# Clustered attention in front of two expert layers: four kinds of operands per head in place of six

## The chip, the cores and the metric

One core of a Trainium2 chip runs the whole program. The metric is the device time of one execution in microseconds (us). Engines: PE (TensorE, matrix products), DVE (VectorE), ACT (ScalarE), POOL (GpSimd), SP (SyncE, which here only issues DMAs).

## The reference

Attention of 2 batches x 8 heads, 768 positions, head size 64. Every query and key belongs to the one of 16 centroids with the largest cosine similarity; a query only sees keys of its own cluster. The result feeds a squared-ReLU layer (512 to 2048 to 512) and then a layer of 8 experts of which each token takes one.

```python
q_assign = argmax(q_n @ c_n.T)            # first of equal maxima
k_assign = argmax(k_n @ c_n.T)
mask = q_assign[:, :, :, None] == k_assign[:, :, None, :]
scores = where(mask, scale * q @ k.T, -1e9)
scores = scores - max(scores, -1)
attn = exp(scores); attn = attn / (sum(attn, -1) + 1e-9)
x = attn @ v
g = s * relu(x @ w_in) ** 2 + b ; y = g @ w_out
out[token] = gate * relu(y @ w1[e]) @ w2[e]     # e: the token's best expert
```

A query whose cluster holds no key has every score at -1e9. All its weights are then equal, and its result is the mean of all values.

## The kernel before

Numbers keep nearly float32 accuracy by being split into two f16 parts, high and low; a product is then three products of parts.

**One head** is prepared in two functions and used in two more. `prep1` (L133) splits K and Q: ACT casts the high parts into `pk1`, POOL subtracts to get the low parts, and a transposing DMA writes `tk1`, with [high; low] of K and of Q on the 128 rows. V is split into `v1` without a transpose. `prep2` (L188) computes similarities to the centroids on PE (`sim`, L198), and on DVE a one-hot row per position: maximum, comparison, weighting by descending index so that of equal maxima the first stays, maximum, comparison (L202 to L210). It then packs `pk2` with four kinds of rows: (0) K high with the keys' one-hot times 32768, (1) Q high twice, (2) Q high with a mask, (3) Q low with the mask. A matmul with ones counts the keys in each cluster (`cnt`, L216); a query whose cluster is empty gets a zero mask and its values are cleared by a bitwise and (L219 to L231), so that its scores come out equal. Kinds 0 to 2 are transposed to `tk2` (18 blocks of 128x128). With the two kinds of `tk1` that makes six.

`unit_max` (L243) computes, for half a head (384 queries), the scores with queries on partitions from high parts alone, in 6 matmuls of 128x384, and takes the row maximum on DVE (L255, L259). The maximum, scaled (L260), becomes one more column of kind 3, which is transposed to `qb`. `unit` (L266) computes for each of 6 key chunks the transposed scores from two accumulating matmuls, `tk1` with `tk2` kind 1 (L287) and `tk2` kind 0 with `qb` (L289); the maximum is subtracted in the second. ACT takes exponentials (L292 and, for chunks that are split into f16 parts, L297), POOL or DVE computes the low part `pl` (L300), and PE multiplies with V (L279). The DVE normalizes (L308 to L313), ACT and POOL write the result split in two (L316, L317).

**Transposes** go by DMA from SP's queue (L115), except for the first head and the centroids, which PE transposes by a product with an identity, in groups of three blocks, copied out alternately by ACT and DVE (L118 to L124).

**The order.** Generators are interleaved: while `unit` of head i walks its chunks, one step each of `unit_max` of head i+1 and `prep2` of head i+2 is issued, and `prep1` of head i+3. The weights of the squared-ReLU layer come as 64-bit numbers and are decoded in 32 chunks (`f64_chunk`: DVE L333, L334, L337, ACT L331, L339, POOL L340). The first chunks are held behind named instructions of head 0 and 1 with `issue_after`, which holds the chunk's instructions of the same engine as the named one; the rest are spread over heads 5 to 11. From head 8 on, steps of the squared-ReLU layer on batch 0 (`moe1`: PE L442 and L456, ACT L445 and L448, DVE L447 and L449) are issued between heads. When the heads are done, the rest of that layer runs, then the experts. The Tile framework puts instructions of each engine into an order by a simulation when it compiles; each engine then works in that order.

Of the kernel before, what the change touches and what calls it, by code (L numbers as in the profile page):

```python
# [43 lines left out]
def tile_kernel(ctx: ExitStack, tc, q, k, v, centroids, w_in, w_out, s, b, w_gate, w1, w2, out, dbg=None):  # L44
# [67 lines left out]
    def transpose(i, dst, src, pools=None):  # L112

        if i not in PE_T:
            nc.sync.dma_start_transpose(out=dst, in_=src.rearrange("p n x -> p (n x)"))  # L115
            return
        for g in range(0, src.shape[1], HC):
            pool, name = ((st_p, "st"), (sm_p, "sm"))[g // HC % 2] if pools is None else pools  # L118
            ps = pool.tile([P, HT], F32, name=name)
            nn = min(HC, src.shape[1] - g)  # L120
            for n in range(nn):
                nc.tensor.matmul(out=ps[:, n * P:(n + 1) * P], lhsT=src[:, g + n], rhs=ident, start=True, stop=True)
            (nc.scalar.copy if g // HC % 2 == 0 else nc.vector.tensor_copy)(
                out=dst[:, g:g + nn], in_=ps[:, 0:nn * P].rearrange("p (n x) -> p n x", n=nn))  # L124
# [8 lines left out]
    def prep1(i):  # L133
        h = hd[i]
        t = h.pop("kqv")
        kq = t[:, 0:2].rearrange("p a (c d) -> p (a c) d", d=D)
        pk1 = pk.tile([P, 2, NC, P], F16, name="pk1")
        kqp = pk1.rearrange("p a c x -> p (a c) x")
        nc.scalar.copy(out=kqp[:, :, 0:D], in_=kq)
        nc.gpsimd.tensor_tensor(out=kqp[:, :, D:2 * D], in0=kq, in1=kqp[:, :, 0:D], op=ALU.subtract)  # L140
        tk1 = tpool(i).tile([P, 2, NC, P], F16, name="tk1")
        transpose(i, tk1.rearrange("p a c x -> p (a c) x"), pk1.rearrange("p a c x -> p (a c) x"))
# [24 lines left out]
    _, wt_c = iota([P, C], [[-1, C]], C, 0, "wt_c")  # L167
# [20 lines left out]
    def prep2(i):  # L188
        bb, hh = heads[i]
        h = hd[i]  # L190
        pk1, tk1 = h.pop("pk1"), h["tk1"]
# [26 lines left out]
        ohq = tmp.tile([P, NC, C], F32, name="ohq")
        nc.vector.scalar_tensor_tensor(out=ohq, in0=cnt.unsqueeze(1).broadcast_to([P, NC, C]), scalar=0.0,  # L219
                                       in1=oh[:, NC:2 * NC], op0=ALU.is_gt, op1=ALU.mult)  # L220
        al = small.tile([P, NC], F32, name="al")
        nc.vector.tensor_reduce(out=al, in_=ohq, axis=AX.X, op=ALU.add)
        alm = small.tile([P, NC], I32, name="alm")
        nc.vector.tensor_scalar(out=alm, in0=al, scalar1=-1.0, scalar2=None, op0=ALU.mult)
        alb = small.tile([P, NC], F32, name="alb")
        nc.vector.tensor_scalar(out=alb, in0=al, scalar1=BIGM, scalar2=None, op0=ALU.mult)
        yield
        nc.vector.scalar_tensor_tensor(out=pk2[:, 2, :, 64:64 + C], in0=ohq, scalar=BIGM,
                                       in1=alb.unsqueeze(2).broadcast_to([P, NC, C]), op0=ALU.mult, op1=ALU.subtract)
        nc.vector.tensor_copy(out=pk2[:, 3, :, 64:64 + C], in_=pk2[:, 2, :, 64:64 + C])  # L230
        nc.vector.tensor_tensor(out=pk2.bitcast(I32)[:, 2:4, :, 0:D // 2],  # L231
                                in0=pk1.bitcast(I32)[:, 1].rearrange("p c (t d) -> p t c d", t=2),
                                in1=alm.unsqueeze(1).unsqueeze(3).broadcast_to([P, 2, NC, D // 2]),
                                op=ALU.bitwise_and)
        yield
# [665 lines left out]
```

## Time and profile before

| | us |
|---|---|
| runs before | 762.03, 757.33, 759.59 (median 759.59) |
| the profiled execution | 756.67 |
| its span in the profile | 754.9 |
| PE busy | 652.6 |
| DVE busy | 573.3 |
| ACT busy | 416.1 |
| POOL busy | 287.7 |
| mean granted clock of PE | 0.962 |

The durations come from one execution. Busy time of an engine is the union of its instructions' times; a matmul's duration holds its latency, so that means of single matmuls are longer than their share of the busy time. In a row of a group, "x16" is the number of instructions, then stand busy us and mean ns, then the idle time of the engine just before them and what ended it. Names such as `pk` stand for all tiles whose name begins so (pk1, pk2).

### The profile page before, as it was taken

Reading aid. Unit: us, or ns where it says so; the run is one execution under the profiler, and the core shown is the slowest. Engines: PE = TensorE matmul, PEld = TensorE weight load, DVE = VectorE, ACT = ScalarE, POOL = GpSimd, SP = SyncE. Lnnn points to the kernel's source line nnn. Section 1 sums busy time; section 2 is a strip of 40 time slices with the busy share of each in tenths; the row PEclk is TensorE's granted clock in tenths of the full one; section 3 lists DMA queues with packets and bytes.
Section 4 is the critical chain, followed back from the end, with each engine's and each line's share of the span. In section 5 each row is a group of like instructions: output and inputs, shape, how many; then the busy total and the mean of one; then the engine's idle time right before and its main releaser. Section 6 shows DMA issues by size and latency. Waiting matters only on the chain.

```text
span 754.9 us, 16103 instructions
## 1 busy us (share of the span) xinstructions
PE 652.6 (86%) x6171; PEld 424.4 (56%) x6171; DVE 573.3 (76%) x1271; ACT 416.1 (55%) x789; POOL 287.7 (38%) x335
## 2 busy tenths in 40 slices
PE   1467876988878889999999999999999889999884
PEld 1235654766544545566555565465476758776661
DVE  8999899979999997789862363276943867877772
ACT  5356566655677655566754252045713566756762
POOL 6346567645756545545434210011013323220101
PEclk9999699989998999999999999999999999999998
DMA  7465667656493345334201500008843378688841
GB/s 228 141 145 143 150 168 160 151 129 131 93 199 117 83 124 107 52 77 74 43 12 44 99 29 1 15 30 293 320 164 87 86 219 293 219 275 209 265 144 48
DMA packets 134482, 101.26 MB, mean 134 GB/s; under 512 B 110332, under 2 KB 116476, under 8 KB 132096
## 3 DMA queue, kind: packets, MB, share of 16 engines
q1 hardware_dynamic: 124304, 68.58, 36.9%
q10 hardware_dynamic: 6576, 22.06, 8.9%
q0 software_dynamic: 3520, 9.54, 3.5%
q8 instruction: 50, 0.82, 0.4%
q14 instruction: 32, 0.26, 0.1%
HBM read 85.05 MB, written 7.39 MB: 122 GB/s over the span
## 4 chain that ended last, share of the span: by engine, by line
PE 40%; DVE 28%; DMA 16%; issue 12%; ACT 2%; SPq 0%; POOLq 0%; POOL 0%; DVEq 0%; ACTq 0%
PE py L456 15%; PE ps L442 10%; DMA out<-o,oid 8%; DVE mxt L255 5%; PE pv L279 4%; PE hps L666 4%; DMA tk<-pk 3%; DVE l L334 2%; DVE r L447 2%; DVE l L333 2%; DVE m L337 2%; DMA raw<-in_moe_w_out 2%; PE st L289 2%; PE st L287 2%; PE sm L252 2%
## 5 line engine op out<-in xcount | busy, mean ns | idle before, releaser
L300 POOL TENSOR_TENSOR pl<-p,ph 128x384 f16<-128x384 f32 x128 | 127.1, 998 | 105.0 <-ACT ph L297 54.2
L442 PE MATMUL ps<-xt,wi 128*128 128x384 f16 x768 | 137.3, 331 | 0.0
L456 PE MATMUL py<-wo,g 128*128 128x512 f16 x576 | 134.0, 382 | 1.6 <-ACT r L445 1.6
L292 ACT ACTIVATE p<-st 128x384 f32<-128x384 f32 x192 | 93.6, 491 | 65.6 <-PE st L289 58.8
L255 DVE TENSOR_REDUCE mxt<-sm 128x1 f32<-128x384 f32 x192 | 102.2, 545 | 16.0 <-PE sm L252 15.5
L442 PEld LDWEIGHTS <-wi 128*128 128x128 f16 x768 | 74.7, 99 | 51.2 <-issue 4.7
L456 PEld LDWEIGHTS <-g 128*128 128x128 f16 x576 | 55.4, 98 | 63.2 <-issue 3.7
L252 PE MATMUL sm<-tk 128*128 128x384 f16 x192 | 64.0, 355 | 29.8 <-DVE mxt L255 27.2
L287 PE MATMUL st<-tk,tk 128*128 128x384 f16 x192 | 66.3, 345 | 7.1 <-ACT ph L297 5.1
L289 PE MATMUL st<-qb,tk 128*128 128x384 f16 x192 | 66.1, 347 | 6.6 <-DMA qb<-pk 6.6
L297 ACT ACTIVATE ph<-st 128x384 f16<-128x384 f32 x144 | 70.3, 489 | 0.0
L448 ACT ACTIVATE g<-r,b 128x384 f16<-128x384 f32 x64 | 39.4, 616 | 50.3 <-DVE r L447 50.3
L686 POOL DMA_INDIRECT out<-o,oid x16 | 22.2, 1385 | 106.3 <-ACT o L685 100.9
L680 PEld LDWEIGHTS <-ht 128*128 128x128 f16 x384 | 36.9, 98 | 42.6 <-issue 1.3
L449 DVE SCALAR_TENSOR_TENSOR g<-r,b,g 128x384 f16<-128x384 f32 x64 | 45.5, 710 | 18.5 <-ACT g L448 18.5
L279 PEld LDWEIGHTS <-ph 128*128 128x128 f16 x864 | 45.9, 101 | 21.9 <-issue 5.8
L523 POOL DMA_INDIRECT yreg<-yp,posi x12 | 12.5, 1042 | 113.1 <-DVE posi L509 87.3
L279 PE MATMUL pv<-v,ph 128*128 128x65 f16 x864 | 53.3, 198 | 1.9 <-ACT ph L297 1.4
L666 PE MATMUL hps<-x2t,wa 128*128 128x128 f16 x768 | 48.7, 227 | 7.0 <-DVE ht L671 4.4
L606 DVE SCALAR_TENSOR_TENSOR wa<-stg,wa 128x1024 f16<-128x1024 f32 x40 | 46.9, 1219 | 8.2 <-ACT wa L605 8.0
L666 PEld LDWEIGHTS <-wa 128*128 128x128 f16 x768 | 46.9, 102 | 9.7 <-issue 5.0
L447 DVE SCALAR_TENSOR_TENSOR r<-r,s 128x384 f32<-128x384 f32 x64 | 47.5, 742 | 1.6 <-ACT r L445 1.6
(219 smaller groups left out, 1264.4 us busy)
## 6 DMA issues: line engine op xcount, KB each, us to landing
stg<-in_moe_w SPq DMA_DIRECT2D x44, 1024.0 KB, 7.7
raw<-in_moe_w_out ACTq DMA_DIRECT2D x16, 512.0 KB
stg<-in_moe_w ACTq DMA_DIRECT2D x8, 1024.0 KB, 7.3
raw<-in_moe_w_in ACTq DMA_DIRECT2D x10, 512.0 KB, 6.0
kqv<-in_k SPq DMA_DIRECT2D x16, 192.0 KB, 3.7
kqv<-in_q SPq DMA_DIRECT2D x16, 192.0 KB, 3.9
kqv<-in_v SPq DMA_DIRECT2D x16, 192.0 KB, 5.6
raw<-in_moe_w_in SPq DMA_DIRECT2D x6, 512.0 KB, 6.1
```

The source lines that it names most:

```text
L252: nc.tensor.matmul(out=sm, lhsT=tk2[:, 2, c0 + c, :], rhs=tk2[:, 0, n * HC:(n + 1) * HC, :].rearrange("p c x -> p (c x)"), start=True, sto ...
L255: nc.vector.tensor_reduce(out=mxt[:, c, n:n + 1], in_=sm, axis=AX.X, op=ALU.max)
L279: nc.tensor.matmul(out=pv[:, c, :], lhsT=p[:, c * P:(c + 1) * P], rhs=w, start=first[0], stop=(kc == NC - 1 and c == HC - 1 and p is parts ...
L287: nc.tensor.matmul(out=st, lhsT=tk1[:, 0, kc, :], rhs=tk2[:, 1, c0:c0 + HC, :].rearrange("p c x -> p (c x)"), start=True, stop=False)
L289: nc.tensor.matmul(out=st, lhsT=tk2[:, 0, kc, :], rhs=qb.rearrange("p c x -> p (c x)"), start=False, stop=True)
L292: nc.scalar.activation(out=p32, in_=st, func=AF.Exp, scale=1.0 / 8.0)
L297: nc.scalar.activation(out=ph, in_=st, func=AF.Exp, scale=1.0 / 8.0)
L300: eng.tensor_tensor(out=pl, in0=p32, in1=ph, op=ALU.subtract)
L442: nc.tensor.matmul(out=ps, lhsT=wi[:, a, kk, f * P:(f + 1) * P], rhs=xt[:, c, kk], start=(kk == 0 and n == 0), stop=(kk == KD - 1 and n == 2))
L447: nc.vector.scalar_tensor_tensor(out=g0, in0=r, scalar=s4, in1=r, op0=ALU.mult, op1=ALU.mult)
L456: st8["py"] = nc.tensor.matmul(out=ps, lhsT=g[:, a, f, c * P:(c + 1) * P], rhs=wo[:, w, f], start=(f == 0 and n == 0), stop=(f == KF - 1 a ...
L666: nc.tensor.matmul(out=ps[:, j], lhsT=ws[:, w, kk * F + f0:kk * F + f0 + P], rhs=xt[:, a, kk], start=(i == 0), stop=(i == 3 * KD - 1))
```

## The change

Operands per head become four kinds: `tk1` holds, per chunk, [K high; K low] and [Q low; Q high], so that one pass gives both cross products; `tk2` holds K high and Q high with their one-hot rows (12 blocks). The high product, mask and maximum come in the second pass. Empty clusters are no longer treated ahead: `unit_max` derives a flag from the row maximum (no key reaches the level of an own cluster), and behind the normalization a predicated copy puts the mean of V, computed by a matmul with ones, into the rows that are flagged. The one-hot chain is in f16 and in one piece; scaling and copying into `pk2`, and the maximum's column, are ACT's. PE transposes write f16 in groups of six.

```diff
-    def transpose(i, dst, src, pools=None):
+    def transpose(i, dst, src, pool=None):
...
+        n0 = 2 * HC
+        for g in range(0, src.shape[1], n0):
+            nn = min(n0, src.shape[1] - g)
+            odd = g // n0 % 2
+            p, name = ((st_p, "st"), (sm_p, "sm"))[odd] if pool is None else pool
+            ps = p.tile([P, n0, P], F16, name=name)
             for n in range(nn):
-                nc.tensor.matmul(out=ps[:, n * P:(n + 1) * P], lhsT=src[:, g + n], rhs=ident, start=True, stop=True)
...
+                nc.tensor.transpose(out=ps[:, n], in_=src[:, g + n], identity=ident)
+            (nc.vector.tensor_copy if odd else nc.scalar.copy)(out=dst[:, g:g + nn], in_=ps[:, 0:nn])
...
-        pk1 = pk.tile([P, 2, NC, P], F16, name="pk1")
...
+        pk1 = pk.tile([P, NC, 4, D], F16, name="pk1")
+        nc.scalar.copy(out=pk1[:, :, 0::3], in_=kq)
+        nc.gpsimd.tensor_tensor(out=pk1[:, :, 1:3], in0=kq, in1=pk1[:, :, 0::3], op=ALU.subtract)
...
-        t = (pk if i < 2 else tpa).tile([P, 4, NC, P], F16, name=f"pk2_{i}", bufs=1)
+        t = (pk if i < 2 else tpa).tile([P, 2, NC, P], F16, name=f"pk2_{i}", bufs=1)
...
+        pk2 = pk2_of(i)
+        nc.scalar.copy(out=pk2[:, :, :, 0:D], in_=pk1[:, :, 0::3].rearrange("p c a d -> p a c d"))
...
-        oh = tmp.tile([P, 2 * NC, C], F32, name="oh")
+        oh = tmp.tile([P, 2 * NC, C], F16, name="oh")
...
-        st8[f"a{i}"] = nc.vector.tensor_scalar(out=pk2[:, 0, :, 64:64 + C], in0=oh[:, 0:NC], scalar1=BIGM, scalar2=None, op0=ALU.mult)
+        st8[f"a{i}"] = nc.vector.tensor_tensor(out=oh, in0=oh, in1=pm.unsqueeze(2).broadcast_to([P, 2 * NC, C]), op=ALU.is_equal)
+        nc.scalar.activation(out=pk2[:, 0, :, 64:64 + C], in_=oh[:, 0:NC], func=AF.Copy, scale=BIGM)
+        st8[f"b{i}"] = nc.scalar.activation(out=pk2[:, 1, :, 64:64 + C], in_=oh[:, NC:2 * NC], func=AF.Copy,
+                                            scale=BIGM, bias=-BIGM)
+        tk2 = tpool(i).tile([P, 2, NC, P], F16, name="tk2", bufs=4 if i < H else 2)
+        transpose(i, tk2.rearrange("p a c x -> p (a c) x"), pk2.rearrange("p a c x -> p (a c) x"))
         yield
...
+        vsp = aux.tile([P, D], F32, name="vsp", tag="aux")
         for c in range(NC):
-            nc.tensor.matmul(out=cnt, lhsT=ones16, rhs=pk2[:, 0, c, 64:64 + C], start=(c == 0), stop=(c == NC - 1))
...
+            for t in range(2):
+                nc.tensor.matmul(out=vsp, lhsT=ones16, rhs=v1[:, c, t, 1:1 + D], start=(c == 0 and t == 0), stop=(c == NC - 1 and t == 1))
+        vm = tmp.tile([P, D], F32, name="vm", bufs=3)
+        nc.scalar.activation(out=vm, in_=vsp, func=AF.Copy, scale=SX / S)
...
-                nc.tensor.matmul(out=sm, lhsT=tk2[:, 2, c0 + c, :],
+                nc.tensor.matmul(out=sm, lhsT=tk2[0:64 + C, 1, c0 + c, :],
...
-        st8[f"c{i}{qh}"] = nc.vector.tensor_scalar(out=pk2[:, 3, c0:c0 + HC, 64 + C], in0=mm1, scalar1=-1.0 / BIGM, scalar2=None,
+        st8[f"c{i}{qh}"] = nc.scalar.activation(out=pk2[:, 1, c0:c0 + HC, 64 + C], in_=mm1, func=AF.Copy, scale=-1.0 / BIGM)
...
+            nc.scalar.activation(out=h["flag"], in_=h["mm1"], func=AF.Relu, scale=-1.0, bias=nokey)
...
-            nc.tensor.matmul(out=st, lhsT=tk1[:, 0, kc, :],
...
+            nc.tensor.matmul(out=st.rearrange("p (c x) -> p c x", c=HC), lhsT=tk1[:, kc, 0, :],
+                             rhs=tk1[:, c0:c0 + HC, 1, :], start=True, stop=False)
...
+        nc.vector.copy_predicated(out=x3, mask=h["flag"][:, qh].bitcast(I32).unsqueeze(2).broadcast_to([P, HC, D]),
+                                  data=h["vm"].unsqueeze(1).broadcast_to([P, HC, D]))
```

With the removed lines go `cnt`, `ohq`, `al`, `alm`, `alb` and all DVE writes of `pk2` behind them (L212 to L238), and four of the six yields of `prep2`.

## Rows read from the trace of the kernel before

**Rows 1.** The page, part 1: busy us, share of the span, instructions

```profile
PE 652.6 (86%) x6171; PEld 424.4 (56%) x6171; DVE 573.3 (76%) x1271; ACT 416.1 (55%) x789; POOL 287.7 (38%) x335
```

**Rows 2.** Busy us of each engine by stage, granted clock, DMA share

```profile
core 0: us, PE busy (x) PEld busy (x) DVE busy (x) ACT busy (x) POOL busy (x), PEclk, DMA share, GB/s
0.00:72.90 72.90, 35.22 (x367) 23.79 (x368) 69.50 (x167) 37.34 (x72) 38.49 (x69) 1.00 0.63 170
72.90:198.60 125.70, 102.27 (x1067) 76.19 (x1067) 115.90 (x297) 77.96 (x178) 77.81 (x86) 0.89 0.62 141
198.60:297.20 98.60, 82.97 (x739) 48.68 (x738) 93.13 (x173) 62.49 (x136) 57.31 (x59) 0.95 0.51 120
297.20:424.70 127.50, 122.99 (x1241) 75.14 (x1238) 87.71 (x243) 72.01 (x173) 59.84 (x72) 0.99 0.29 58
```

**Rows 3.** The chain of waits within 72.9 to 198.6 us, its shares by line

```profile
by line: DVE mxt L255 13.8%; PE pv L279 9.7%; issue 6.9%; DMA qb<-pk 6.1%; DVE pk L236 5.5%; PE sm L252 4.2%; DVE l L333 4.1%; PE st L289 4.1%; PE st L287 3.9%; DMA kqv<-in_v 3.7%; DMA tk<-pk 3.6%; DMA raw<-in_moe_w_out 3.5%; DVE pk L230 2.
```

**Rows 4.** The same stages and columns, instructions that write or read pk alone

```profile
0.00:72.90 72.90, 5.75 (x60) 3.55 (x36) 14.58 (x29) 4.14 (x5) 11.23 (x9) 1.00 0.63 170
72.90:198.60 125.70, 2.49 (x42) 0.00 (x0) 31.93 (x60) 6.68 (x8) 12.27 (x7) 0.89 0.62 141
198.60:297.20 98.60, 0.59 (x12) 0.00 (x0) 12.44 (x18) 1.66 (x2) 4.92 (x3) 0.95 0.51 120
...
L182 DVE MEMSET pk<- x2: 698/698/698, 1.1 to 1.9; 128x768 uint32 x2
```

**Rows 5.** Groups of DVE instructions on the cluster counts, first and last

```profile
L219 DVE SCALAR_TENSOR_TENSOR ohq<-cnt,oh 128x96 f32<-128x96 f32 x16 | 3.9, 244 | 0.4 <-PE cnt L216 0.3
...
L226 DVE TENSOR_SCALAR alb<-al 128x6 f32<-128x6 f32 x16 | 2.5, 159 | 0.0
```

**Rows 6.** DVE writers of pk: ns shortest/median/longest, start of first and last

```profile
L212 DVE TENSOR_SCALAR pk<-oh x16: 192/210/1160, 18.2 to 356.3; 128x96 f16<-128x96 f32 x16
...
L236 DVE COPY pk<-pk x16: 344/936/1797, 23.8 to 363.3; 128x768 f16<-128x768 f16 x16
...
L260 DVE TENSOR_SCALAR pk<-mm x32: 153/164/1397, 37.9 to 394.2; 128x3 f16<-128x3 f32 x32
```

**Rows 7.** Groups by form on DVE: arithmetic over 128x192 and a mask

```profile
L206 DVE TENSOR_TENSOR oh<-oh,wt_c 128x192 f32<-128x192 f32 x16 | 8.4, 528 | 0.1
...
L231 DVE TENSOR_TENSOR pk<-pk,alm 128x384 int32<-128x384 int32 x16 | 12.6, 788 | 0.0
...
L313 DVE TENSOR_TENSOR x<-pv,rec 128x192 f32<-128x192 f32 x32 | 11.1, 347 | 0.1
```

**Rows 8.** Groups by form on ACT, three widths

```profile
L139 ACT CAST pk<-kqv 128x768 f16<-128x768 f32 x16 | 13.3, 832 | 8.8 <-DVE pk L231 8.7
L316 ACT CAST xp<-x 128x192 f16<-128x192 f32 x32 | 11.3, 353 | 14.5 <-DVE x L313 14.3
L361 ACT ACTIVATE r<-n 128x1 f32<-128x1 f32 x1 | 0.2, 203 | 0.0
```

**Rows 9.** Groups by form on PE, two narrow products

```profile
L279 PE MATMUL pv<-v,ph 128*128 128x65 f16 x864 | 53.3, 198 | 1.9 <-ACT ph L297 1.4 <-DVE x L313 0.3
L216 PE MATMUL cnt<-pk,ones 128*128 128x16 f16 x96 | 5.3, 173 | 8.2 <-DVE pk L212 8.2
```

**Rows 10.** Busy us over heads 6 and 7, columns as in rows 2

```profile
166.70:198.60 31.90, 26.42 (x323) 19.59 (x322) 30.21 (x86) 20.50 (x48) 20.29 (x22) 1.00 0.53 106
```

**Rows 11.** Waits within stage 1: us in total, times, longest

```profile
ACT p L292 <- PE st L289: 25.4, 26, 2.6
...
ACT xp L316 <- DVE x L313: 9.1, 7, 3.1
```

**Rows 12.** The table load in front of the first exponential

```profile
L292 ACT ACT_TABLE_LOAD x1 | 1.3, 1283 | 0.0
```

**Rows 13.** SP's transposing DMAs into tk: ns shortest/median/longest

```profile
L115 SPq DMA_TRANSPOSE tk<-pk x30: 1334/2450/3739, 11.0 to 366.3; - x30
```

More of the change, by code (lines that the diff above doesn't have):

```diff
@@ L135, in prep1 @@
         t = h.pop("kqv")
-        kq = t[:, 0:2].rearrange("p a (c d) -> p (a c) d", d=D)
-        pk1 = pk.tile([P, 2, NC, P], F16, name="pk1")
[L138 to L142, printed above, removed]
+        kq = t[:, 0:2].rearrange("p a (c d) -> p c a d", d=D)
+        pk1 = pk.tile([P, NC, 4, D], F16, name="pk1")
+        nc.scalar.copy(out=pk1[:, :, 0::3], in_=kq)
+        nc.gpsimd.tensor_tensor(out=pk1[:, :, 1:3], in0=kq, in1=pk1[:, :, 0::3], op=ALU.subtract)
+        tk1 = tpool(i).tile([P, NC, 2, P], F16, name="tk1")
+        transpose(i, tk1.rearrange("p c a x -> p (c a) x"), pk1.rearrange("p c (a t) d -> p (c a) (t d)", t=2))
         v1 = tpool(i).tile([P, NC, 2, D + 1], F16, name="v1")
@@ L165, in iota @@
         return ti, tf
-    _, wt_c = iota([P, C], [[-1, C]], C, 0, "wt_c")
+    _, wt32 = iota([P, C], [[-1, C]], C, 0, "wt32")
+    wt_c = const.tile([P, C], F16, name="wt_c")
+    nc.vector.tensor_copy(out=wt_c, in_=wt32)
+    nokey = const.tile([P, 1], F32, name="nokey")
+    nc.gpsimd.memset(nokey, -BIGM * BIGM / 2)
     ones16 = const.tile([P, P], F16, name="ones16")
@@ L190, in prep2 @@
         h = hd[i]
-        pk1, tk1 = h.pop("pk1"), h["tk1"]
+        pk1, tk1, v1 = h.pop("pk1"), h["tk1"], h["v1"]
+        pk2 = pk2_of(i)
+        nc.scalar.copy(out=pk2[:, :, :, 0:D], in_=pk1[:, :, 0::3].rearrange("p c a d -> p a c d"))
         sim = aux.tile([P, 2 * NC, C], F32, name="sim", tag="aux")
@@ L218, in prep2 @@
[L218 to L234, printed above, removed]
@@ L235, in prep2 @@
[L235 to L241 removed]
+        nc.vector.tensor_tensor(out=oh, in0=oh, in1=wt_c.unsqueeze(1).broadcast_to([P, 2 * NC, C]), op=ALU.mult)
@@ L243, in unit_max @@
+        nc.scalar.activation(out=vm, in_=vsp, func=AF.Copy, scale=SX / S)
+        h.update(pk2=pk2, tk2=tk2, qb={}, vm=vm)
     def unit_max(i, qh):
@@ L257, in unit_max @@
                     yield
-        mm1 = small.tile([P, HC], F32, name="mm1")
+        if not qh:
+            h["mm1"] = small.tile([P, 2, HC], F32, name="mm1")
+        mm1 = h["mm1"][:, qh]
         nc.vector.tensor_reduce(out=mm1, in_=mxt, axis=AX.X, op=ALU.max)
-        st8[f"c{i}{qh}"] = nc.vector.tensor_scalar(out=pk2[:, 3, c0:c0 + HC, 64 + C], in0=mm1, scalar1=-1.0 / BIGM, scalar2=None,
-                                op0=ALU.mult)
+        st8[f"c{i}{qh}"] = nc.scalar.activation(out=pk2[:, 1, c0:c0 + HC, 64 + C], in_=mm1, func=AF.Copy, scale=-1.0 / BIGM)
         qb = tpool(i).tile([P, HC, P], F16, name="qb")
-        transpose(i, qb, pk2[:, 3, c0:c0 + HC, :])
+        transpose(i, qb, pk2[:, 1, c0:c0 + HC, :])
         h["qb"][qh] = qb
+        if qh:
+            h["flag"] = small.tile([P, 2, HC], F32, name="flag")
+            nc.scalar.activation(out=h["flag"], in_=h["mm1"], func=AF.Relu, scale=-1.0, bias=nokey)
         yield
```

27 lines of the change are left out of this document (4 added, 23 removed).

## Prediction

> **What bounds the kernel now.** I read the page's busy shares first [rows 1]: TensorE (PE) 652.6 us of 754.9, VectorE (DVE) 573.3. Averages over the span hide that the bound changes, so I cut the span where heads end (the normalization of each half head, L313, marks the ends) and read the busy time of each engine per stretch [rows 2]. Stage 0 (to 72.9 us: load, first preparations, head 0): DVE 69.50 of 72.90. Stage 1 (to 198.6: heads 1 to 7): DVE 115.90 of 125.70, PE 102.27 at a granted clock of 0.89, ScalarE (ACT) 77.96. Stage 2 (to 297.2: heads 8 to 10, with the first products of the squared-ReLU layer and the decoding of its second weights): DVE 93.13 of 98.60, PE 82.97. Stage 3 (to 424.7: heads 11 to 15): PE 122.99 of 127.50, DVE 87.71. What follows never sees the attention; I let it move as a block. The chain of waits of stage 1 [rows 3] says the same: the DVE's score maxima lead it (13.8%), and copies of the preparation into `pk` stand in it (L236 5.5%).
>
> So DVE work taken away before 297 us should be worth something, after it nearly nothing. 2 preparations run ahead, so 13 of the 16 lie in stages 0 to 2 (about 3.3, 7 and 3).
>
> **VectorE, removed.** All DVE instructions that write `pk1`/`pk2` go (one-hot scaling, the masked copies, duplicates, the two row-maximum scalings per head). Their busy time by stage is one view [rows 4]: 14.58, 31.93 and 12.44 us. Of the 14.58, two memsets of 0.70 us are no such work; half of them is saved by the smaller buffer, which leaves 13.8 (rounded down for two memsets of single columns). Besides, four small instructions on the cluster counts go (244 + 240 + 419 + 159 ns = 1.06 us a head, first and last shown [rows 5]): 3.5, 7.4 and 3.2 us. Removed: 17.3, 39.3, 15.6.
>
> **VectorE, added.** One predicated copy per half head, 128x192 f32. No row has the operation. The nearest are two arithmetic passes over the same shape: 347 ns with one input in PSUM, 528 ns with both in SBUF [rows 7]. I take the middle, 0.44 us, and keep 0.35 and 0.79 as ends (the latter is the integer mask that it resembles, over twice the width [rows 7]). 2, 14 and 6 of them: 0.9, 6.2, 2.6 us. The one-hot chain's reductions and comparisons stay; in f16 they may get shorter, which I leave at zero gain (bound: 0.2 us for each of two, 5 us in 13 heads). Head 0's transposes on PE leave PSUM in fewer, wider pieces, and a third fewer blocks of one operand: counted at nothing, and no more than what stage 0 is left open by below. Net relief: 16.4, 33.1 and 13.0 us, 62.5 in all.
>
> **ScalarE, added.** Per head a 128x768 f16 copy, for which a cast of that size is the row: 832 ns [rows 8]. The two one-hot writes (128x96), the mean of V (128x64), two row maxima (128x3) and the flag (128x6) lie between 203 ns for one element and 353 ns for 192 [rows 8], so 0.28, 0.28, 0.25 and three of 0.21. Sum 2.27 us; ends 1.9 and 2.8. In stage 1: 7 x 2.27 = 16 on 78, which is 94 of what was 125.7: covered as long as the stage is longer than about 100 us. No table load is charged: the only one behind the first exponential is its own [rows 12], although Relu and Copy follow it.
>
> **TensorE.** The score passes keep their number and width; the maximum pass only uses fewer rows. The count's six matmuls (5.3 us for 96, 55 ns each) go, and twelve 128x64 ones for the sum of V come, for which the 128x65 passes are the row (53.3 us for 864, 62 ns each) [rows 9]: +0.41 us a head, ends 0 and 0.8. It is on the path only in stage 3: +1.2 us.
>
> **Queues.** The second transposing DMA of a head moves 12 blocks instead of 18; SP's issue of these took 1.33 to 3.74 us with a median of 2.45 [rows 13], so about 1.2 us less for SP and for the transfers behind it (loads of K, Q, V; the `qb` transposes). The old preparation yields six times, the new one twice, so the transposed operand is in the program earlier. I value both at zero; if covered work shows, up to 3 us gain. The wait hooks of weight chunks 2, 4 and 5 now hang on ACT instructions and hold only ACT's part of a chunk. DVE can start its first shift earlier; it waits for ACT's part in the next instruction anyway. Zero, ends -2 and +2.
>
> **Why a copy costs more than its work.** In the rows the f16 copy of 128x768 took 344 ns at best and 936 at its median, and a 128x96 scaling 192 to 1160 [rows 6]; ACT's cast stays at 832. [...]
>
> **The sum by stages.** Stage 1 after: DVE 82.8, ACT 94, PE 105. What will it take? Two heads there without weight decoding took 31.9 us with DVE at 30.2, PE 26.4, ACT 20.5 [rows 10]: 15.95 us a head, still DVE-bound, so 7 heads take at most 112 (-14). If instead PE fills the 92% that DVE fills now, 13.2/0.92 = 14.4 a head, 100.5 (-25). I take the middle, 106.5: -19. Stage 0: DVE is full, but the new chain goes through ACT, PE and a DMA, and waits of that chain already stand beside the DVE; of 16.4 I take 9 (ends 3 and 16.4). Stage 2: PE 83 + 1.2 is next; at the DVE's 94.5% that is 89, at most -9.5, and the DVE keeps the weight decoding; I take 6 (end 0). Stage 3: +1.2 on PE against 4.5 us of idle PE that may shrink: 0 (ends -3 and +2). Total -34. The profiled execution took 756.67 us (span 754.9), the median of the runs is 759.59. 756.67 - 34 = 722.7; carried over to the median, 725.6. Forecast 726 us.
>
> **Rivals.**
> 1. More: all of the relief in stage 0 (-16.4), PE-filled stages 1 and 2 (-25, -9.5), -3 in stage 3: -54, 706 us. For it: stages 0 to 2 have the DVE over 92% busy. Against: three engines end within 15% of each other.
> 2. The waiting moves on: if the long times of the removed copies are waits for a port which the next DVE instruction would then do, only their shortest durations are gained. The eleven lines' minima (first, a long one and the last shown [rows 6]; the row-maximum scaling twice) add up to 2.79 us a head, less two predicated copies of at least 0.34: 2.1, times 13 = 27.5 of the 62.5. Gain 34 x 27.5/62.5 = 15: 744 us. [...]
> 3. PE is the bound already in stages 1 and 2 in the sense that its gaps are latency between engines (in stage 1 the exponentials waited for PE 25.4 us [rows 11]). Then the DVE's relief turns into waiting: -5 to 0, about 756 us.
> 4. Slower: ACT works in order and now waits for DVE in three places a head: the one-hot writes and both row maxima. Behind each stand exponentials that free the two score buffers PE writes. ACT's existing wait of this kind (the normalized rows) cost 9.1 us in 7 times, 1.3 each [rows 11]. All on the path: 13 x 3 x 1.3 = 51, less 34: +17, 776 us. It decides from 34/39 = 0.87 us a wait. Against: DVE is shorter, so its results are later than ACT less often.
>
> **Chances.** Forecast (gain 20 to 45) 0.54; rival 1 0.10; rival 2 (8 to 20) 0.19; rival 3 0.09; rival 4 0.08. A measurement tells 1%, 7.6 us, from no change: nearly all of rival 2 counts as faster, so 0.80 faster, 0.12 within 1%, 0.08 slower. The range takes in rivals 1 and 2 and stops at -1%: 704 to 752.
>
> **What would show it.** DVE busy down by about 72 us over the span (65 to 85), ACT up by about 36 (30 to 45), PE up by 3 to 8; stage 1 near 107 us with PE or ACT, not DVE, over 85%; stage 3 and what follows as long as now; the predicated copy between 0.35 and 0.79 us. ACT rows of the one-hot or the row maxima with long idle before them, ended by DVE, would be rival 4; a weight-decoding or comparison row on DVE whose mean has grown would be rival 2; DVE well under 80% in stage 1 at an unchanged length rival 3. I am wrong if stage 0 to 2 shorten by less than 20 us in sum, or if stage 3 grows by what they gain.

## The result, and the profile after

Over four runs the changed kernel took 739.86 us in the median (737.16 to 740.95), the kernel before, run beside it, 758.47 (757.33 to 762.03): a ratio of 0.9734, 95% interval 0.969 to 0.9779. That is faster, by 18.6 us of the 34 that were forecast. The profiled execution took 740.1 us, its span is 738.4. Ratios and medians, here and below, are of fast executions; two kernels of the experiments also had slow ones (two and three of ten), which are left out.

Part 1 of the page of the kernel after, beside [rows 1]:

```profile
PE 654.7 (89%) x6261; PEld 426.1 (58%) x6261; DVE 525.0 (71%) x1109; ACT 436.2 (59%) x897; POOL 293.5 (40%) x336
```

PE's work is what it was (+2.1 us). DVE's busy time fell by 48.3 us (forecast 72), ACT's rose by 20.1 (forecast 36).

The stages, cut where the same heads end (0, 7, 10, 15), beside [rows 2]; the columns are those of rows 2:

```profile
0.00:65.20 65.20, 37.78 (x367) 25.45 (x368) 58.31 (x134) 43.41 (x96) 39.00 (x71) 1.00 0.80 192
65.20:182.10 116.90, 102.67 (x1119) 77.58 (x1119) 93.00 (x218) 82.93 (x220) 73.93 (x85) 0.88 0.57 130
182.10:282.10 100.00, 82.93 (x762) 49.08 (x762) 86.25 (x148) 66.92 (x158) 62.77 (x60) 0.93 0.47 120
282.10:415.00 132.90, 129.74 (x1295) 79.03 (x1294) 82.81 (x227) 77.78 (x199) 59.49 (x74) 1.00 0.25 53
```

Stage 0 went from 72.9 to 65.2 us (-7.7), stage 1 from 125.7 to 116.9 (-8.8), stage 2 from 98.6 to 100.0. Stage 3 is 5.4 longer, but its end is no good mark: work of the squared-ReLU layer moves across it. That layer's own end (the first product of the experts) is: 556.8 us before, 540.0 after. From head 8 to there is one stretch, in the kernel before

```profile
198.60:556.80 358.20, 338.06 (x2779) 195.16 (x2778) 255.18 (x605) 187.66 (x400) 129.77 (x149) 0.98 0.38 100
```

and after

```profile
182.10:540.00 357.90, 337.66 (x2820) 195.76 (x2821) 241.53 (x554) 196.85 (x445) 133.90 (x150) 0.98 0.36 98
```

DVE has 14 us less to do in it, and it is as long as it was: PE is busy for 94% of it in both. The whole gain of the profiled execution lies ahead of head 8.

Within stage 1 the gain is not spread evenly either. Head 1, head 2, and heads 3 to 7 of the kernel before (the same view):

```profile
72.90:94.70 21.80, 17.40 (x142) 12.98 (x142) 18.75 (x45) 13.25 (x29) 13.06 (x16) 0.69 0.56 132
94.70:114.90 20.20, 15.81 (x168) 11.61 (x165) 20.20 (x45) 11.51 (x26) 14.23 (x16) 0.92 0.67 164
114.90:198.60 83.70, 69.06 (x765) 51.60 (x764) 76.95 (x210) 53.21 (x123) 50.52 (x55) 0.94 0.63 137
```

and of the kernel after:

```profile
65.20:87.70 22.50, 19.49 (x156) 14.57 (x156) 17.24 (x39) 13.42 (x35) 12.54 (x15) 0.62 0.55 124
87.70:110.40 22.70, 17.91 (x178) 12.84 (x177) 21.20 (x39) 16.46 (x41) 16.31 (x20) 0.85 0.72 174
110.40:182.10 71.70, 65.27 (x791) 50.16 (x791) 54.56 (x143) 53.05 (x146) 45.08 (x52) 0.98 0.53 118
```

Heads 3 to 7 fell from 83.7 to 71.7 us: 14.3 a head, the better end of the forecast (14.4), with DVE busy for 76% of it and PE for 91%. Heads 1 and 2 gave 3.2 us back: 42.0 before, 45.2 after. DVE's work in these two did not fall: 38.95 us before, 38.44 after. In head 1 DVE is busy for 17.24 of 22.5 us and PE for 19.49, at a granted clock of 0.62.

How head 1 begins can be read on DVE's timeline (start, duration, line), kernel after:

```profile
66.06 1.79 DVE L330 SCALAR_TENSOR_TENSOR m<-raw,l 128x512 uint32<-128x512 uint32 x1
67.78 1.07 DVE L306 COPY_PREDICATED x<-flag,vm 128x192 f32<-128x192 int32 x1
68.76 1.01 DVE L242 TENSOR_REDUCE mxt<-sm 128x1 f32<-128x384 f32 x2
```

and on PE's, where the bracket holds the idle time and what ended it:

```profile
67.49 0.33 PE L280 MATMUL st<-qb,tk 128*128 128x384 f16 x1
69.36 0.48 PE L239 MATMUL sm<-tk 80*128 80x384 f16 x1 [1.54 <-DVE mxt L242]
70.63 0.48 PE L278 MATMUL st<-tk 128*128 128x384 f16 x1 [0.80 <-ACT p L283]
```

On DVE's timeline each instruction starts about where the one ahead of it ends. A decoding step that took 1.79 us and the new predicated copy, 1.07, stand ahead of the maximum that frees PE's score buffer; PE idles 1.54 us. It then idles another 0.80 us for ACT, which had been held up too, by a chunk of weights that had not landed and whose first step stands ahead of the exponential:

```profile
69.53 0.68 ACT L324 ACTIVATE m<-raw 128x512 f32<-128x512 f32 x1 [3.95 <-DMA raw<-in_moe_w_in]
```

The products behind take 0.48 us where they took 0.33. PE's granted clock is 1.00 up to 68 us, 0.63 from 68 to 70 and 0.50 from 70 to 84. So two waits stand ahead of this fall, one for a lump in DVE's order and one for a DMA that stalls ACT. The kernel before had a fall of the clock in the same place, behind a third kind of wait:

```profile
73.91 0.48 PE L289 MATMUL st<-qb,tk 128*128 128x384 f16 x1 [1.92 <-DMA qb<-pk]
```

There the clock is 0.50 from 74 to 80 us. Whether a wait lowers the clock, which one, and whether the longer low stretch after the change comes from the predicated copy, one timeline of each cannot tell.

### The profile page after: what moved, and what is told of

It reads as the page before. It is cut to its first block, busy times and chain, and to the rows that moved or that the text cites. A ratio compares the mean times of both kernels' runs of the same rounds, so it can differ in the third digit from the quotient of the medians.

```text
span 738.4 us, 16238 instructions
## 1 busy us (share of the span) xinstructions
PE 654.7 (89%) x6261; PEld 426.1 (58%) x6261; DVE 525.0 (71%) x1109; ACT 436.2 (59%) x897; POOL 293.5 (40%) x336
## 5 line engine op out<-in xcount | busy, mean ns | idle before, releaser
L435 PE MATMUL ps<-xt,wi 128*128 128x384 f16 x768 | 135.3, 330 | 5.7 <-DMA xt<-xp 4.1
L449 PE MATMUL py<-wo,g 128*128 128x512 f16 x576 | 132.2, 382 | 0.0
L239 PE MATMUL sm<-tk 80*128 80x384 f16 x192 | 64.5, 363 | 17.1 <-DVE mxt L242 11.9
L278 PE MATMUL st<-tk 128*128 128x384 f16 x192 | 65.6, 342 | 7.4 <-ACT ph L288 4.6
L679 POOL DMA_INDIRECT out<-o,oid x16 | 26.9, 1682 | 103.4 <-ACT o L678 94.6
L280 PE MATMUL st<-qb,tk 128*128 128x384 f16 x192 | 65.8, 343 | 0.0
L659 PE MATMUL hps<-x2t,wa 128*128 128x128 f16 x768 | 45.7, 219 | 3.8 <-DVE wa L599 1.5
L659 PEld LDWEIGHTS <-wa 128*128 128x128 f16 x768 | 43.7, 98 | 6.8 <-issue 2.0
L440 DVE SCALAR_TENSOR_TENSOR r<-r,s 128x384 f32<-128x384 f32 x64 | 43.4, 678 | 4.2 <-ACT r L438 4.0
```

The source lines that it names most:

```text
L239: nc.tensor.matmul(out=sm, lhsT=tk2[0:64 + C, 1, c0 + c, :], rhs=tk2[0:64 + C, 0, n * HC:(n + 1) * HC, :].rearrange("p c x -> p (c x)"), s ...
L278: nc.tensor.matmul(out=st.rearrange("p (c x) -> p c x", c=HC), lhsT=tk1[:, kc, 0, :], rhs=tk1[:, c0:c0 + HC, 1, :], start=True, stop=False)
L280: nc.tensor.matmul(out=st, lhsT=tk2[:, 0, kc, :], rhs=qb.rearrange("p c x -> p (c x)"), start=False, stop=True)
L435: nc.tensor.matmul(out=ps, lhsT=wi[:, a, kk, f * P:(f + 1) * P], rhs=xt[:, c, kk], start=(kk == 0 and n == 0), stop=(kk == KD - 1 and n == 2))
L449: st8["py"] = nc.tensor.matmul(out=ps, lhsT=g[:, a, f, c * P:(c + 1) * P], rhs=wo[:, w, f], start=(f == 0 and n == 0), stop=(f == KF - 1 a ...
L659: nc.tensor.matmul(out=ps[:, j], lhsT=ws[:, w, kk * F + f0:kk * F + f0 + P], rhs=xt[:, a, kk], start=(i == 0), stop=(i == 3 * KD - 1))
```

## The experiments

Each kernel was run against the kernel before on the same chip. The changed kernel is the base unless said otherwise; "layer end" is the first expert product in the profiled execution, which lies up to 7 us from the median of its kernel, so that single ends are good to a few us.

| edit | DVE busy | median us (before beside it) | ratio, 95% interval | layer end |
|---|---|---|---|---|
| kernel before | 573.3 | 758.47 | 1 | 556.8 |
| kernel after | 525.0 | 739.86 (758.47) | 0.9734 [0.969, 0.9779] | 540.0 |
| copies back on DVE | 549.6 | 739.66 (763.27) | 0.970 [0.9631, 0.9768] | 543.7 |
| the same, and scratch load | 576.8 | 758.29 (763.70) | 0.992 [0.9881, 0.9959] | 559.0 |
| kernel before, copies to ACT | 558.2 | 758.06 (763.70) | 0.9933 [0.989, 0.9975] | 551.7 |
| an extra transposing DMA | 527.3 | 740.33 (763.70) | 0.9707 [0.9648, 0.9766] | 540.0 |
| one-hot chain in four pieces | 527.8 | 742.5 (759.0) | 0.9757 [0.9696, 0.9818] | 546.5 |
| ACT's copy written later | 524.3 | 739.26 (763.27) | 0.971 [0.9638, 0.9782] | 539.3 |
| no predicated copy | 514.0 | 741.65 (763.27) | 0.9757 [0.9669, 0.9844] | 540.3 |
| no sum of V | 527.9 | 744.42 (759.0) | 0.9796 [0.9745, 0.9846] | 548.2 |
| no product with V's low part | 527.9 | 745.28 (763.27) | 0.9791 [0.9716, 0.9866] | 542.4 |
| layer's first product held | 529.6 | 748.56 (763.70) | 0.9827 [0.9764, 0.989] | 547.9 |
| short decode | 501.7 | 731.44 (759.0) | 0.9649 [0.9579, 0.9719] | 525.7 |
| short decode, copies on DVE | 523.4 | 739.65 (761.76) | 0.9699 [0.9647, 0.975] | 545.4 |

### Which part of the change carries the gain

**Copies back on DVE.** The diff is one kind of edit, four times (the copy of K and Q into `pk2`, both one-hot writes, the row maximum):

```diff
-        nc.scalar.copy(out=pk2[:, :, :, 0:D], in_=pk1[:, :, 0::3].rearrange("p c a d -> p a c d"))
+        nc.vector.tensor_copy(out=pk2[:, :, :, 0:D], in_=pk1[:, :, 0::3].rearrange("p c a d -> p a c d"))
```

> The changed kernel with the K and Q copies into pk2, both one-hot writes and the row-maximum column back on VectorE; everything else as changed. Theory A (the gain comes from VectorE work taken off the stages before head 10, and what moved to ScalarE is covered there): VectorE busy up by about 2.5 us a head (0.94 + 2 x 0.43 + 2 x 0.39, the means of such rows before the change), some 33 us up to head 10, and 6 to 12 us of the gain lost, so 746 to 752 us. Rival C (ScalarE's waits for VectorE eat part of the gain): at or below the changed kernel, 733 to 740 us.

Measured: 0.970, DVE busy +24.6 us. Nothing is lost: theory A's 746 to 752 us did not come, and 739.66 lies in rival C's range. Moving these copies to ACT is worth nothing in this kernel; what is left of the change gives the whole gain. Its first two stages:

```profile
0.00:69.80 69.80, 39.79 (x384) 26.77 (x385) 65.80 (x153) 39.25 (x79) 40.28 (x72) 1.00 0.74 184
69.80:184.30 114.50, 98.08 (x1100) 75.59 (x1099) 100.54 (x250) 75.52 (x184) 73.24 (x85) 0.90 0.60 136
```

Stage 0 is 4.6 us longer than after the change and stage 1 is 2.4 us shorter, although DVE has 7.5 us more to do in each.

**Scratch load.** The same kernel, and in `prep2` the DVE instructions on cluster counts and masks that the change had removed, with the old shapes, writing to scratch tiles that nothing reads (the first reads SBUF where the old one read PSUM). The order of the rest of the program, transposes and operands are those of the change.

```diff
+        nc.vector.scalar_tensor_tensor(out=ohq, in0=oh[:, 0:NC], scalar=0.0, in1=oh[:, NC:2 * NC], op0=ALU.is_gt, op1=ALU.mult)
+        nc.vector.tensor_reduce(out=al, in_=ohq, axis=AX.X, op=ALU.add)
...
+        nc.vector.tensor_copy(out=sc4, in_=sc3[:, 0].unsqueeze(2).broadcast_to([P, NC, 2, D]))
```

> The run with the copies back on VectorE, and besides the eight VectorE instructions per head that the change removed outright (counts, masks, masked copies), with the same shapes and types, on scratch tiles that nobody reads; the operands, transposes and the program's shape stay those of the change. VectorE busy should come to 575 to 590 us, at or above the kernel before. Theory A' (it is VectorE's load that held stages 0 and 1, and the relief counted only down to the point where the next bound stands, so that the copies alone showed nothing): the gain is gone, 752 to 762 us. Rival D (the gain comes from the shape of the preparation: a shorter chain, operands earlier, 12 blocks in the DMA in place of 18): 738 to 745 us.

Measured: 0.992. Its stages 0 and 1:

```profile
0.00:68.00 68.00, 38.27 (x358) 25.17 (x359) 62.37 (x174) 34.92 (x71) 34.55 (x68) 1.00 0.69 170
68.00:196.10 128.10, 107.54 (x1133) 82.34 (x1132) 120.40 (x305) 80.48 (x192) 80.95 (x90) 0.85 0.57 129
```

Stage 1 is as long as before the change (128.1, then 125.7), with DVE at 94% again. Against its base, the run with the copies back on DVE (0.970), 27.2 us of work that does nothing cost 0.022 of 760 us, 16.7: 0.6 us for each us, 0.4 to 0.8 by the two intervals. So most of the gain is DVE's load; at 0.992 some 3 to 9 us of it remain. In stage 0 the load did not come back (DVE is busy for 62.37 us there, 69.50 before the change, 65.80 in the base), so its 68.0 us decide nothing about that stage.

**The kernel before, with three of its DVE writers on ACT** (L212, L238, L260 of the kernel before):

```diff
-        nc.vector.tensor_copy(out=pk2[:, 0, :, 0:D], in_=pk1[:, 0, :, 0:D])
+        nc.scalar.copy(out=pk2[:, 0, :, 0:D], in_=pk1[:, 0, :, 0:D])
```

> The kernel before with one copy per head of K's high part, the keys' one-hot write and both row-maximum columns moved from VectorE to ScalarE, nothing else. VectorE busy down by 25 to 28 us. Theory A' (VectorE is full there, so each us taken off counts until the next bound): 4 to 10 us less, a ratio of 0.987 to 0.995. Rival D: 0.996 to 1.005. ScalarE's waits (rival C): above 1.005.

Measured: 0.9933, that is 5.1 us for 15.1 us of relief, where 25 to 28 had been expected. The interval reaches into rival D's range, so this run alone is weak. Its first two stages:

```profile
0.00:76.40 76.40, 38.33 (x387) 26.71 (x388) 64.96 (x162) 42.57 (x92) 38.79 (x70) 0.96 0.62 163
76.40:187.60 111.20, 93.00 (x1042) 70.23 (x1039) 107.08 (x265) 78.75 (x197) 75.60 (x85) 0.95 0.67 152
```

Stage 0 takes 76.4 us with DVE at 65.0, where the changed kernel with its copies on DVE takes 69.8 with DVE at 65.8: with the old, longer preparation the first head is not held by DVE's load alone. Nor does that load alone order the lengths of stage 1: here it takes 111.2 us with DVE busy for 107.1, less than the changed kernel's 116.9 with 93.0.

**Shape.** Three edits ask whether the fewer blocks of the DMA or the order of the preparation count: an extra transposing DMA of six blocks a head, the one-hot chain cut by three more `yield`s as before, and ACT's copy written behind the similarity products (an edit that should do nothing).

```diff
+        if i not in PE_T:
+            tkx = tpool(i).tile([P, NC, P], F16, name="tkx", bufs=2)
+            transpose(i, tkx, pk2[:, 1])
```

> The changed kernel with one more transposing DMA of 6 blocks per head into a scratch tile, behind the one of 12: as many blocks as before the change. Theory A': within 4 us of the changed kernel (736 to 744). If the fewer blocks carry the gain (a part of rival D): 746 to 755 us.

> The changed kernel with the one-hot chain in four pieces again (three more yields in the preparation), so that its instructions and the transpose are issued later in the program. Theory A': the same load in another order, within 4 us of the changed kernel (736 to 744). Rival D (operands that come earlier carry the gain): 746 us or more.

> The changed kernel with the ScalarE copy into pk2 written behind the similarity matmuls in the program instead of ahead of them: the same instructions on every engine, perhaps in another order. It measures what the order that the framework draws up is worth by itself. All theories: within 3 us of the changed kernel; if it is 5 us or more away, differences of that size between the other runs are not to be read as the effect of their edit.

Measured: 0.9707, 0.9757 and 0.971, all within the interval of the changed kernel. Neither the DMA nor the pieces carry it, as theory A' said.

### What holds the kernel after the change

**No predicated copy** (rows of empty clusters are left as they come):

```diff
-        nc.vector.copy_predicated(out=x3, mask=h["flag"][:, qh].bitcast(I32).unsqueeze(2).broadcast_to([P, HC, D]),
-                                  data=h["vm"].unsqueeze(1).broadcast_to([P, HC, D]))
```

> The changed kernel without the predicated copy (rows of empty clusters are left as they are). Theory A: VectorE loses 32 x 0.68 = 21.8 us, 14 of it before head 10, but stages 0 and 1 are now held by TensorE with its low granted clock, so the time falls by 0 to 5 us (735 to 740). Rival B (VectorE is still the bound through its longer waits beside GpSimd): 8 to 14 us less (726 to 732), and the weight-decoding row that went from 825 to 980 ns goes back.

Measured: 0.9757. The operation has 21.8 us of DVE time in the changed kernel, and without it nothing is gained; DVE's busy time falls by 11.0 us only. The last decoding step took 0.90 us on average in its 27 instances from 40 us on, where the changed kernel's 27 took 0.99 and the 28 of the kernel before 0.82: half of the way back. Its stage 1:

```profile
70.20:185.40 115.20, 101.20 (x1108) 78.08 (x1109) 86.59 (x204) 84.39 (x220) 73.66 (x84) 0.89 0.60 131
```

The granted clock is 0.89 with the copy gone and 0.88 with it, so the copy as such is not what holds the clock of this stage down.

**Less work on PE.** Once without the twelve products for the sum of V (ACT copies rows of V in its place), once without the product of the exponentials with V's low part (432 matmuls fewer):

```diff
-                late.append((kc, [(ph, [v1[:, kc, 0], v1[:, kc, 1]]), (pl, [v1[:, kc, 0]])]))
+                late.append((kc, [(ph, [v1[:, kc, 0]]), (pl, [v1[:, kc, 0]])]))
```

> The changed kernel without the twelve products for the sum of V (left out; the mean is taken from one row). TensorE loses 16 x 0.72 = 11.5 us, of which 6 behind the start of head 8. If TensorE's sum of work sets the length from head 8 on: 4 to 7 us less there, 733 to 736 us. If the filler between the heads only runs out earlier, as in the run without V's low part: 737 to 743 us.

> The changed kernel without the product of the high weights with the low part of V (left out): 18 matmuls a head less in batch 0 and 36 in batch 1, at 62 ns 1.1 and 2.2 us. Theory A (TensorE holds the program from head 1 on): stage 1 shorter by 5 to 8 us, the stages from head 8 on by 14 to 18, about 717 us. Rival B: stage 1 as long as now, only the later 14 to 18 us, about 724 us.

Measured: 0.9796 and 0.9791: not faster, though there is less to do, and longer than every range that was expected. The second one's first two stages did get shorter:

```profile
0.00:63.70 63.70, 37.08 (x346) 24.82 (x347) 57.18 (x133) 42.38 (x93) 38.10 (x70) 1.00 0.80 194
63.70:174.20 110.50, 96.67 (x991) 71.85 (x989) 93.41 (x218) 83.54 (x220) 75.30 (x85) 0.91 0.58 138
```

Stage 1 is 6.4 us shorter than after the change with DVE's work the same (93.41 and 93.00), within the 5 to 8 that theory A gave: there the work on PE counts. From head 8 to the layer's end it is all given back:

```profile
174.20:542.40 368.20, 339.08 (x2538) 190.06 (x2539) 244.34 (x554) 199.07 (x448) 131.51 (x151) 0.95 0.38 95
```

282 matmuls fewer than after, and PE is busy for 339.1 us (337.7 after), at a clock of 0.95 (0.98). What the removed products freed came back as a lower clock and as idle time (29 us, after 20). Near 411 us PE waited 2.73 us for the input of the squared-ReLU layer; that the layer's work which used to fill such gaps had been used up earlier is a reading of the timeline, not shown by a run of its own.

**The layer's first product held** behind head 8, to see whether the squared-ReLU layer, started early, gets in the heads' way:

```diff
+                    with tc.issue_after(st8["s811"].ins) if (bb, qh, f, kk, n) == (0, 0, 0, 0, 0) else nullcontext():
```

> The changed kernel with the squared-ReLU layer's first product held behind a score product of head 8's second half on TensorE. In the changed kernel TensorE waited 4.1 us there for the transposed input, had work of head 8 queued behind, and then ran at half clock. Theory E (the gain that failed to come in stage 2 is that exposed chain at the batch boundary, which VectorE's backlog used to cover): 4 to 7 us less than the changed kernel, 733 to 736 us. If from head 8 on the length is set by VectorE's decoding or by TensorE's sum of work: within 2 us, 738 to 742.

Measured: 0.9827. Its four executions (747.4 to 752.49 us) all lie above those of the extra DMA (738.91 to 742.03) beside the same runs of the kernel before, so it is slower than the changed kernel. That idea fell: held back, the layer's products are missed there; started early, they are not an obstacle.

**Short decode.** One shift in place of two DVE instructions a weight chunk; the three lowest mantissa bits of the decoded weights are left out.

```diff
-        nc.vector.tensor_scalar(out=l, in0=raw[:, :, 0], scalar1=29, scalar2=None, op0=ALU.logical_shift_right)
-        nc.vector.scalar_tensor_tensor(out=l, in0=m.bitcast(U32), scalar=3, in1=l,
-                                       op0=ALU.logical_shift_left, op1=ALU.bitwise_or)
+        nc.vector.tensor_scalar(out=l, in0=m.bitcast(U32), scalar1=3, scalar2=None, op0=ALU.logical_shift_left)
```

> The changed kernel with a shorter decoding of the 64-bit weights: per chunk one VectorE shift in place of a shift and a combining instruction; the three lowest bits of the decoded mantissas are left out. VectorE loses some 0.8 us a chunk, 13 us up to head 7 and 13 behind it. Theory A' (stage 1 is past the point where VectorE's load counts): nothing there; if VectorE's decoding holds stage 2 (it was 100% busy in most of it), 5 to 8 us less, all between head 8 and head 10: 732 to 735 us. If what follows head 8 is TensorE's sum of work: within 2 us, 738 to 742.

Measured: 0.9649, the lowest ratio of all, though its interval overlaps the changed kernel's. Its stages 0 to 2, from the shortest of its four executions:

```profile
0.00:59.20 59.20, 36.91 (x349) 24.80 (x349) 49.43 (x126) 41.97 (x93) 35.69 (x69) 1.00 0.83 208
59.20:171.30 112.10, 96.95 (x1137) 75.66 (x1138) 85.02 (x208) 83.54 (x220) 73.20 (x87) 0.92 0.62 140
171.30:266.90 95.60, 82.16 (x760) 49.14 (x757) 78.69 (x133) 68.65 (x161) 59.90 (x61) 0.96 0.52 125
```

Against the changed kernel that is 6.0 us less in stage 0 for 8.9 us less work on DVE, 4.8 in stage 1 for 8.0, and 4.4 in stage 2 for 7.6. The total is about what was expected, the place is not: theory A' had put the gain of stage 1 at nothing.

**Short decode and copies on DVE**, the last run, joins two edits measured singly:

> This joins two edits that were measured singly: e1's copies and scalings back on VectorE (DVE busy +25 us, time unchanged) and e14's decode with one VectorE instruction fewer per weight chunk (DVE busy -23 us, ratio 0.965; as there, the three lowest mantissa bits of the decoded weights are left out). DVE busy should come out within 5 us of the changed kernel's 525. Theory load (what counts is how much VectorE has to do before 280 us): the two cancel, the ratio is that of the changed kernel, 0.971 to 0.976 (about 740 us). Theory place (a decode chain is a lump in VectorE's order in front of the score maxima; work of the preparation is hidden): e14's gain stays whole, ratio 0.962 to 0.967 (about 731 us), with stage 0 near 60 to 63 us and stage 1 near 112.

Measured: 0.9699 [0.9647, 0.975], with DVE busy 523.4. The ratio lies just outside what the load theory gave (0.971 to 0.976) and further from the place theory's 0.962 to 0.967; the interval reaches into both. Its first two stages

```profile
0.00:64.00 64.00, 38.20 (x366) 25.12 (x367) 57.07 (x143) 38.62 (x78) 38.18 (x72) 1.00 0.80 198
64.00:179.40 115.40, 96.68 (x1120) 74.71 (x1119) 93.38 (x239) 76.20 (x186) 73.66 (x85) 0.94 0.58 130
```

are near the changed kernel's (65.2 and 116.9, DVE 58.31 and 93.00), not the short decode's. So load is the better reading, but this run does not settle it.

**All runs together.** Two pairs differ in DVE's load almost alone. With the scratch load the layer's end goes from 543.7 us (DVE busy 549.6) to 559.0 (576.8), 0.56 us for each us; in the kernel before, with three writers on ACT, from 556.8 (573.3) to 551.7 (558.2), 0.34. From 549.6 down to 514 the end lies between 539 and 548 whatever the load; some of these edits change the order and some the work of PE, and their effects are not told apart. The short decode, 501.7, goes lower again, in stages 0 and 1 by 10.8 us for 16.9 us less work on DVE. So no one curve over DVE's load fits all runs. What is shown is that the work which the change removed from DVE had cost about 0.6 us for each us, and that the copies moved to ACT returned nothing; why the two differ is open.

## Why the prediction was right, and where its steps failed

The sign, the mechanism and the place were right: most of the gain came out of DVE's load (the scratch load took most of it back), it lies in stages 0 and 1, and what follows stayed. 739.86 us lies in the range of 704 to 752, which was wide enough to take in two rivals. The size was not right: 18.6 us instead of 34, outside the forecast's own band of 20 to 45 and in the second rival's (8 to 20), for another main reason than the rival's. By the prediction's own sign it was wrong: stages 0 to 2 shortened by 15.1 us in sum, less than the 20 that it named. Nor did the busy times of DVE, ACT and PE change by what it gave.

**Net relief of DVE, 62.5 us in the stages and 72 over the span.** Measured 41.0 in the stages (11.2, 22.9 and 6.9) and 48.3 over the span. The forecast added up durations and compared the sum with busy time, which is a union. The groups' durations of DVE add up to 646.2 us before and 581.3 after: 64.9 less, near the forecast. But consecutive DVE instructions overlap by some hundredths of a us: the sum is 72.9 us above the busy time before and 56.3 after, so the removed ones had overlapped their neighbours. On ACT likewise: the groups' sum rose from 462.6 to 499.8, by 37.2 (forecast 36), the union by 20.1.

The sum itself falls short by 7.1 us; two terms stand out. Groups by form of the kernel after, beside [rows 7, 8] (busy us, mean ns, idle before):

```profile
L306 DVE COPY_PREDICATED x<-flag,vm 128x192 f32<-128x192 int32 x32 | 21.8, 683 | 0.3
L330 DVE SCALAR_TENSOR_TENSOR m<-raw,l 128x512 uint32<-128x512 uint32 x32 | 31.4, 980 | 0.4
L211 DVE TENSOR_TENSOR oh<-oh,wt_c 128x192 f16<-128x192 f16 x16 | 9.2, 575 | 0.2
L214 DVE TENSOR_TENSOR oh<-oh,pm 128x192 f16<-128x192 f16 x16 | 8.6, 537 | 0.1
L197 ACT COPY pk<-pk 128x768 f16<-128x768 f16 x16 | 13.3, 831 | 9.0 <-DMA qb<-pk 8.0 <-issue 1.1
L215 ACT ACTIVATE pk<-oh 128x96 f16<-128x96 f16 x16 | 4.7, 291 | 4.2 <-DVE oh L214 4.2
L249 ACT ACTIVATE pk<-mm 128x3 f16<-128x3 f32 x32 | 7.1, 221 | 4.0 <-DVE mm L248 3.9
L225 PE MATMUL vsp<-v,ones 128*128 128x64 f16 x192 | 11.5, 215 | 5.2 <-DVE oh L210 5.1
```

The predicated copy took 0.68 us, not 0.44, inside the bounds of 0.35 and 0.79: 7.8 us more. The last decoding step, in the kernel before

```profile
L337 DVE SCALAR_TENSOR_TENSOR m<-raw,l 128x512 uint32<-128x512 uint32 x32 | 26.4, 826 | 0.3
```

has grown to 980 ns, 5.0 us in all: the second rival's sign, but 5 of the 35 us that the rival needs. Shorter rows elsewhere (the squaring of the layer, 742 ns before and 678 after, 4.1 us in all) make up for most of it. ACT's terms were right: the copy 831 ns (832 forecast; with the copies back on DVE it took 463 there), the row maximum 221, the one-hot writes 291 and 282. PE's was as well: twelve products for the sum of V cost 60 ns each (62 forecast).

**Stage 1, -19 forecast, -8.8 measured.** This is the term that failed. It was carried over from heads 6 and 7 [rows 10], two heads without weight decoding at a granted clock of 1.00, to all seven. Heads 1 and 2 had taken 42.0 us before, not twice 15.95, at clocks of 0.69 and 0.92, and the trace of before showed it. In them DVE was not relieved, for decoding moved into them. DVE's work on the decoding's tile `l` (its three steps), heads 1 and 2 and then heads 3 to 7, in the kernel before

```profile
72.90:114.90 42.00, 13.25 (x16) 0.80 0.61 147
114.90:198.60 83.70, 8.56 (x11) 0.94 0.63 137
```

and after:

```profile
65.20:110.40 45.20, 19.09 (x21) 0.74 0.64 149
110.40:182.10 71.70, 2.39 (x3) 0.98 0.53 118
```

5.8 us more in heads 1 and 2, 6.2 less in heads 3 to 7. So it is partly luck that heads 3 to 7 came out at the forecast's 14.3 us a head: of the 22.4 us by which DVE's work fell in them, over a quarter is decoding that ran earlier. The prediction put the weight chunks' new hooks at zero; that they are what moved the decoding was not isolated. The forecast that PE or ACT, not DVE, would be over 85% came true (PE 88%, DVE 80%); that this stage would be 107 us did not.

PE's busy time in stage 1 times its granted clock is 91.0 us before, 90.3 after, and between 88 and 92 in all the runs above whose stage 1 is printed: PE's work in it hardly changes. The clock alone does not set the length: the last run had 0.94 and took 115.4 us, the short decode 0.92 and 112.1. That DVE's lumps are what lets the clock fall is read from one timeline, in which ACT's wait for weights stands beside them, and was not isolated; a kernel that keeps PE busy in these gaps with products nobody needs was not tried.

**Stage 0, -9 forecast, -7.7 measured.** Right in size, for a relief of 11.2 us and not 16.4. How much of it is DVE's load and how much the shorter preparation of the first head is open: the scratch load did not bring the load of this stage back, and the kernel before with less load there took 3.5 us longer, not less.

**Stage 2, -6 forecast, +1.4 measured.** DVE's share fell from 94.5% to 86%, PE's busy time stayed (82.97 and 82.93), and the time stayed with it. The step failed that PE could be filled to 94.5%: the stretch is one with what follows, to the layer's end, and there PE is at 94% already. Why stage 2 itself holds 17 us of idle PE is open. Without the product with V's low part it took 105.3 us and with the layer held 103.0; only the two edits with the short decode made it shorter by more than 2 us (95.6 and 97.4).

**The rivals.** Against the first, the prediction held that three engines end within 15% of each other; by its own sums of stage 1 (82.8, 94 and 105) the ends are 27% apart. The fourth, waits on ACT, is small: waits of the row maximum and the one-hot writes came to 3.9 and 4.2 us over the whole run, where the rival charged 51. With the copies back on DVE they are gone and the time is the same, so that these waits ate a gain of that size is not excluded. The third (PE's gaps are latency) was not seen as it was put: the stage got shorter, and the longest wait of [rows 11] nearly halved, as did PE's wait for the score maxima. That wait before, and waits of stage 1 after, in the columns of rows 11:

```profile
PE sm L252 <- DVE mxt L255: 9.4, 12, 2.5
...
ACT p L283 <- PE st L280: 13.5, 16, 2.1
...
PE sm L239 <- DVE mxt L242: 4.5, 4, 1.7
...
ACT xp L309 <- DVE x L306: 3.3, 4, 0.9
```

The score maximum took 545 ns before and 546 after (519 to 558), while one instance of the decoding step took from 674 to 2011 ns. By the timelines of after, ten instances of the decoding step had no POOL instruction beside them and took 0.67 to 0.69 us; the other 22 took 0.68 to 2.01, 1.12 on average. The maximum kept its time beside POOL (0.55 on average with and without). It reads PSUM and the decoding step two tiles in SBUF, but a reduction that reads SBUF, the one-hot chain's over 128x192 (L213), took 334 to 353 ns in all its 16 instances. What the longer instances wait for, a port as in the second rival or something else, no trace names.

## What to carry to other kernels

What relief of a busy engine is worth has to be measured part by part: put the load back on scratch tiles, and move single parts back (here the removed work counted at 0.6 us for each us, and the moves to ACT were worth nothing). Look at where other work goes when an engine gets free: decoding that moves earlier makes one head look better and another worse. Compare a sum of durations with a sum of durations and a busy time with a busy time, and carry a row of one head only to heads that run at the same granted clock and beside the same work. In an order that is shared by several layers, less work on the engine that is full need not be faster (here two such edits were not).

## What the runs showed of the hardware that was not expected

- A predicated copy of 128x192 f32 took 363 ns at the shortest, 618 at the median and 1316 at the longest; the multiplication of the same shape in front of it, which reads PSUM, 350 on average.
- The one-hot chain's means did not fall in f16 where both inputs lie in SBUF and one is broadcast: 575 and 537 ns after, 528 and 524 before. In its shortest instances the weighting is faster in f16 (ns shortest/median/longest, before and after); the comparison behind it is not (341 and 342 at the shortest).

```profile
L206 DVE TENSOR_TENSOR oh<-oh,wt_c x16: 341/358/1226, 16.6 to 352.2; 128x192 f32<-128x192 f32 x16
L211 DVE TENSOR_TENSOR oh<-oh,wt_c x16: 241/318/1589, 14.6 to 332.5; 128x192 f16<-128x192 f16 x16
```

- Scaling the row maximum, 128x3, took 221 ns on ACT and, with the copies back on DVE, 406 on average there (388 before), where the shortest of before was 153 [rows 6]: the engine with the shorter single time was on average the slower place for a small instruction among others.
- Executions of one kernel differ by more than 1%, and the mean granted clock does not always order them: the short decode took 726.6 and 727.7 us at 0.972 and 0.979, and 735.2 twice at 0.963 and 0.969, but the changed kernel 737.16 at 0.972 and 739.61 at 0.976. Differences under 1% between single executions of two kernels are within that.
